# A fused attention and feed-forward kernel: the planner that orders its instructions gets another model of VectorE and GpSimd, new costs and new ranks

## The chip, the core and the metric

The kernel runs on one core of a Trainium2 chip. Its time is the device time of one execution in microseconds (us). The engines are named as the profile names them: PE is TensorE's matmul, PEld its weight load, DVE is VectorE, ACT is ScalarE, POOL is GpSimd, SP is SyncE, which issues most DMAs.

## What is computed

```python
def _attn_ref(q, k, v, n_sink, window):        # (4, 8, 768, 64) each
    scores = np.matmul(q, k.transpose(0, 1, 3, 2)) / np.sqrt(D)
    keep = (pos < n_sink) | ((rel >= 0) & (rel < window))     # 4 sinks, window 128
    scores = np.where(keep, scores, -1e9)
    a = np.exp(scores - np.max(scores, axis=-1, keepdims=True))
    a = a / (np.sum(a, axis=-1, keepdims=True) + 1e-09)
    return np.matmul(a, v)

def _moe_ref(x, w_in, w_out):                  # (3072, 512), (512, 2048), (2048, 512)
    h = np.maximum(x @ w_in, 0.0)
    return (h * h @ w_out).astype(np.float32)
```

The attention's output, with its heads side by side, is the input of the two matrix products.

## The kernel before

The 3072 tokens are cut into eight chunks of 384, two for each batch entry. For each chunk there are four head pairs; one pair of one chunk is one attention step `s` (s = 4 x chunk + pair). An attention step makes scores on PE (line 663 for the first eight steps, 669 with split operands for the others), masks and reduces them on DVE (646, with its accumulator read), takes exponentials on ACT (652), a reciprocal on DVE (712), scales P with it (719, on POOL, ACT or DVE), copies the sink columns into PSK (730 and 732), turns P (by PE, line 849, for chunks 0 and 1; by DVE's 32 x 32 transposes, line 878, and a DMA round trip `via`, lines 889 and 895, for the others) and multiplies with the values (942 and 948). The result is taken out of PSUM as a rounded part `xh` (ACT, 958), a remainder `xl` (DVE, 963) and a 16-bit copy `x16` (515 on POOL, 512 on ACT or DVE).

The products go by columns of 128 of the 2048 hidden units. A column of a chunk has 12 matmuls of the first product (line 1031), then ReLU, square and 16-bit casts on ACT, DVE and POOL (1045, 1050, 1135 or 1133, 512 or 515, and the remainder `gl` on DVE at 1067), then 9 matmuls of the second product (1086 and 1109). The columns are done in nine legs: chunk 0's first 8 columns, chunk 1's 16, chunk 0's other 8, then chunks 2 to 7 with 16 each. So the 33rd column is chunk 2's first.

The weights come as 64-bit numbers in 32 rows. Each row is built into 32-bit and 16-bit parts by three integer steps and one subtraction on DVE (393, 400, 407, 433), a scaling on ACT (428) and a 16-bit cast on POOL, ACT or DVE (441, 512). All this happens while the first two and a half legs run; it is called the building stage here. Chunks 3 to 7 carry side work: their columns reload weights and values in pieces and test their size (`check_steps`, `value_steps`). At the end a few DVE steps form a verdict (`numbers`, `limits`, `within`, `verdict`), which decides whether a general second program has to run.

The order is not written by hand. `Plan.add` records each step with its engine (or a list of engines to choose from), a cost, a rank, what it reads and writes and the PSUM banks it takes. `Plan.order` then simulates the engines: at each point it gives every ready step a start time, picks by time and rank, and emits. A cost of the form `("DVE", 0.62, "port")` marks a DVE operation that shares something with POOL. In the kernel before, a POOL step waits for the marked DVE operation before it (`half`), while a marked DVE operation waits only for a POOL step that carries the mark itself:

```python
                if "port" in kind:
                    t = max(t, port["DVE" if e == "POOL" else "POOL"])
                elif e == "POOL":
                    t = max(t, half)
```

What comes out is a fixed order on each engine; the chip then runs each engine's list in that order, with waits where one needs another.

Of the kernel before, what the change touches and what calls it, by code (L numbers as in the profile page):

```python
# [19 lines left out]
P = 128  # L20
# [4 lines left out]
TOK = 384  # L25
# [9 lines left out]
SHARE = 1.0  # L35
LOW_POOL = 0.57
KLOW_DVE = 0.0
KLOW_POOL = 0.0
HOLD = 0.1
SC_DVE = 0.13  # L40
CLAIM = (True, False)
KS_ACT = 0.01
SOON = 7.71
PS_DVE = 0.19
EARLY = 5
SLOW = 8.5
LAG = 0.77
KEEP = 1.11
STAY = 0.03
LANDS = (3.3, 1.65, 0.6)  # L50
VS_POOL = 3.0
GRAB = 1.9
# [3 lines left out]
URGE = 0.52  # L56
LOW_DVE = 0.0
CP_DVE = 0.47
SC_ACT = 0.26
ROW = 2  # L60
# [5 lines left out]
SHORT_ACT = 0.1  # L66
SHORT_DVE = 0.3
G16_ACT = 0.1
G16_DVE = 0.2
FULL_DVE = 3.0  # L70
# [20 lines left out]
class Plan:  # L91
# [46 lines left out]
    def order(self):  # L138
        free = dict(PE=FIRST, DVE=4.9, ACT=5.1, POOL=5.2, SP=1.7, Q=0.0)
        port, landed, mode, flow, half = {"DVE": 0.0, "POOL": 0.0}, [], 0, 0.0, 0.0  # L140
        open_ = [n for n, s in enumerate(self.steps) if s["waits"] == 0]
        while open_:
            best = {}
            for n in open_:
                s = self.steps[n]
                ready, picks = self.able(s)
                if ready is None:
                    continue
                e, cost, *kind = min(s["at"], key=lambda o: max(ready, free[o[0]]) + o[1] + (o[3] if len(o) > 3 else 0.0))
                t = max(ready, free[e])  # L150
                if e == "SP" and len(landed) > 7:
                    t = max(t, landed[-8])
                if "port" in kind:
                    t = max(t, port["DVE" if e == "POOL" else "POOL"])
                elif e == "POOL":
                    t = max(t, half)
                best.setdefault(e, []).append((t, s["rank"], n, cost, kind, picks))
            chosen = None
            for e, able in best.items():
# [6 lines left out]
                if chosen is None or a[0] < chosen[1][0] or (e == "POOL" and a[0] <= chosen[1][0] + 0.001):  # L166
                    chosen = e, a
            e, (t, rank, n, cost, kind, picks) = chosen
# [15 lines left out]
            else:  # L184
                done = t + cost + self.TAIL[e]
                if "port" in kind:
                    port[e] = t + cost
                    if e == "DVE":
                        half = t + SHARE * cost
# [17 lines left out]
def sink_window_attention_moe(  # L207
# [25 lines left out]
    with ExitStack() as fast:  # L233
# [146 lines left out]
        def row_steps(n, rank):  # L380
# [4 lines left out]
            def load():  # L385
# [6 lines left out]
                ("DVE", 0.345, "port"), rank,  # L392
# [6 lines left out]
                ("DVE", 0.62, "port"), rank,  # L399
# [6 lines left out]
                ("DVE", 0.62, "port"), rank,  # L406
# [6 lines left out]
        def split_steps(n, rank):  # L413
# [6 lines left out]
            def rooms(at):  # L420
# [11 lines left out]
                ("DVE", 0.62, "port"), rank,  # L432
# [6 lines left out]
            def short(e):  # L439
# [4 lines left out]
                [("POOL", 0.65), ("ACT", 0.52, "", SHORT_ACT), ("DVE", 0.36, "port", SHORT_DVE)], rank, short,  # L444
# [6 lines left out]
        def check_steps(n, rank, n_tick):  # L451
# [9 lines left out]
                ("ACT", 0.5), rank,  # L461
# [14 lines left out]
        def scale_steps(fc, rank, n_tick):  # L476

            add(
                ("DVE", 1.2), rank,
# [6 lines left out]
        def value_steps(s, rank, n_tick):  # L486

            half, p = divmod(s, NPAIR)
            kb, nk = 4 * half, 2 if half else 4
# [4 lines left out]
                lambda: nc.sync.dma_start(out=room()[:, 0:nk], in_=v[0, p, :, kb : kb + nk].rearrange("p n x d -> p n (x d)")),  # L494
# [11 lines left out]
        NPS = 2 * NPAIR  # L506
        HALVES = ((0, slice(0, D), slice(D, P)), (1, slice(D, P), slice(0, D)))
# [35 lines left out]
        def attention(s, rank):  # L543
# [68 lines left out]
            if not plain:  # L612
                for h, own, oth in HALVES:
# [3 lines left out]
                        [("DVE", 0.35, "port", 0.0), ("ACT", 0.6 if nk == 4 else 0.5, "", KS_ACT)], r,  # L617
# [18 lines left out]
                        ("DVE", 0.585, "port"), r,  # L636
# [44 lines left out]
            for m, (i, heads) in enumerate(order):  # L681
# [16 lines left out]
                for h, key in zip(heads, keys):  # L698
                    add(
                        ("DVE", 0.355 if n > P else 0.21), r - URGE,  # L700
# [6 lines left out]
                        ("ACT", 0.505 if n > P else 0.385), r - URGE, lambda h=h, i=i, n=n, o=o: exp(h, i, n, o),  # L707
# [27 lines left out]
            for heads in groups:  # L735
# [3 lines left out]
                    ("ACT", 0.2), r - URGE,  # L739
# [802 lines left out]
```

## Time and profile before

| what | before |
|---|---|
| time, median of 3 runs | 653.4 us (653.38 to 653.88) |
| time of the profiled execution | 653.41 us |
| its span from first to last instruction | 651.5 us |
| PE busy | 636.6 us (98%) |
| DVE busy | 483.1 us (74%) |
| ACT busy | 436.2 us (67%) |
| POOL busy | 195.5 us (30%) |
| DMA read and written | 80.29 and 24.38 MB |

The profiled execution is as long as the median. Its time stands 1.9 us over its span. Busy shares are means over stages that have different limits, so they have to be read stage by stage; and PE's ends are modelled, so that a PE that is shown as busy need not be at its full rate.

### The profile page before, as it was taken

What the parts mean: (1) busy time and instruction counts of PE and PEld (TensorE: products, weight loads), DVE (VectorE), ACT (ScalarE), POOL (GpSimd) and SP (SyncE); (2) the same over time, 40 slices, a digit from 0 to 9 for tenths busy, and PEclk for the clock granted to TensorE, in tenths of its full rate; (3) what the DMA queues carried; (4) which work ended last, traced back from release to release, by engine and by line L of the source; (5) the groups of instructions that cost most, each with busy time, mean ns of one, the idle gap of its engine ahead of it and who ended that gap; (6) DMA issues with size and microseconds to landing.
All of it is one profiled execution on the core that took longest, in us unless ns stands there. A gap on an engine that the chain in (4) does not pass through costs nothing.

```text
span 651.5 us, 12170 instructions
## 1 busy us (share of the span) xinstructions
PE 636.6 (98%) x3736; PEld 422.2 (65%) x3736; DVE 483.1 (74%) x1315; ACT 436.2 (67%) x1361; POOL 195.5 (30%) x391
## 2 busy tenths in 40 slices
PE   7989999999999999999999999999999999999995
PEld 6656556665666666666666666666666666666663
DVE  8999999999668676666878776576777888553332
ACT  6998867677675566665568777776777686555421
POOL 4534544636322232323233222333422422000000
PEclk8999999999999999999999999999999999999998
DMA  8636564766766554365677776657667755332001
GB/s 292 219 127 185 173 208 125 232 180 167 198 187 183 127 165 108 92 187 143 181 204 214 217 213 190 197 165 191 187 182 203 222 153 163 116 109 69 17 2 52
DMA packets 85748, 106.53 MB, mean 164 GB/s; under 512 B 12760, under 2 KB 60376, under 8 KB 85676
## 3 DMA queue, kind: packets, MB, share of 16 engines
q1 hardware_dynamic: 85068, 105.05, 55.9%
q8 instruction: 30, 0.49, 0.3%
q10 hardware_dynamic: 576, 0.60, 0.3%
q14 instruction: 42, 0.34, 0.2%
q0 software_dynamic: 32, 0.05, 0.0%
HBM read 80.29 MB, written 24.38 MB: 161 GB/s over the span
## 4 chain that ended last, share of the span: by engine, by line
PE 80%; DVE 12%; ACT 2%; issue 2%; DMA 2%; POOL 1%; SPq 0%; DVEq 0%; ACTq 0%
PE bank L1031 33%; PE bank L1086 23%; PE bank L1109 11%; PE bank L942 5%; PE bank L669 5%; DVE wc L433 2%; DVE f L407 2%; DVE f L400 2%; DVE P L646 1%; PE bank L663 1%; DMA via<-T 1%; DVE f L393 1%; PE bank L948 1%; DVE gc L1067 1%; ACT P L652 1%
## 5 line engine op out<-in xcount | busy, mean ns | idle before, releaser
L1031 PE MATMUL bank<-xc,wc 128*128 128x384 f16 x1024 | 196.2, 327 | 0.6 <-DVE wc L433 0.6
L1031 PE MATMUL bank<-xh,wh 128*128 128x384 f32 x512 | 146.6, 386 | 0.0
L1045 ACT ACTIVATE r<-bank 128x384 f32<-128x384 f32 x128 | 62.6, 489 | 114.6 <-PE bank L1031 89.8
L1031 PEld LDWEIGHTS <-wc 128*128 128x128 f16 x1024 | 90.7, 98 | 67.4 <-issue 9.2
L719 POOL TENSOR_SCALAR P<-P,small 128x260 f32<-128x260 f32 (+1 forms) x158 | 84.8, 551 | 145.0 <-DVE small L712 138.9
L652 ACT ACTIVATE P<-P,nbs 128x260 f32<-128x260 f32 (+1 forms) x192 | 93.2, 486 | 43.6 <-DVE nbs L646 43.1
L1086 PE MATMUL bank<-wc,gc 128*128 128x512 f16 x450 | 110.2, 381 | 0.0
L1135 DVE SCALAR_TENSOR_TENSOR bank<-bank,r 128x384 f32<-128x384 f32 x96 | 54.1, 563 | 63.7 <-ACT r L1045 63.5
L1031 PEld LDWEIGHTS bank<-xh,wh 128*128 128x128 f32 x512 | 90.9, 189 | 13.1 <-ACT P L652 0.3
L1109 PE MATMUL bank<-wc,gc 128*128 128x512 f16 (+1 forms) x350 | 90.9, 364 | 0.4 <-DVE gc L1067 0.4
L646 DVE CUSTOM_DVE_ANT_0 P<-bank,maskA 128x260 f32<-128x260 f32 x128 | 52.6, 420 | 36.4 <-PE bank L669 35.3
L1086 PEld LDWEIGHTS <-gc 128*128 128x128 f16 x450 | 38.0, 98 | 52.8 <-issue 9.4
L1109 PE MATMUL bank<-wh,gh 128*128 128x512 f32 (+1 forms) x175 | 71.4, 445 | 0.2 <-DVE ob L1141 0.2
L1067 DVE TENSOR_TENSOR gc<-bank,gh 128x384 f16<-128x384 f32 x128 | 70.2, 548 | 0.7 <-ACT bank L1133 0.3
L1050 ACT ACTIVATE gh<-r 128x384 fp32r<-128x384 f32 x128 | 66.5, 520 | 3.3
L669 PE MATMUL bank<-KS,QS 128*128 128x260 f32 (+1 forms) x288 | 65.1, 310 | 0.5 <-DVE nbs L646 0.5
L1086 PE MATMUL bank<-wh,gh 128*128 128x512 f32 x225 | 64.8, 396 | 0.0
L669 PEld LDWEIGHTS bank<-KS,QS 128*128 128x128 f32 x288 | 52.2, 189 | 10.0 <-DVE nbs L646 1.2
L878 DVE STREAM_TRANSPOSE T<-P 128x384 f32<-128x384 f32 x96 | 46.8, 495 | 1.8 <-POOL P L719 1.0
L1109 PEld LDWEIGHTS <-gc 128*128 128x128 f16 x350 | 23.9, 98 | 34.6 <-issue 20.7
L515 POOL CAST gc<-gh 128x384 f16<-128x384 f32 x33 | 21.5, 651 | 65.8 <-ACT gh L1050 65.6
L1086 PEld LDWEIGHTS bank<-wh,gh 128*128 128x128 f32 x225 | 38.8, 188 | 3.2
(132 smaller groups left out, 919.2 us busy)
## 6 DMA issues: line engine op xcount, KB each, us to landing
raw<-in_moe_w_dram SPq DMA_DIRECT2D x32, 512.0 KB, 4.3
half<-in_moe_w_dram SPq DMA_DIRECT2D x64, 256.0 KB, 3.1
via<-T SPq DMA_DIRECT2D x96, 96.0 KB, 2.0
PT<-via SPq DMA_DIRECT2D x24, 384.0 KB, 4.2
via<-T SPq DMA_DIRECT2D x96, 80.0 KB, 2.6
PT<-via SPq DMA_DIRECT2D x24, 320.0 KB, 3.8
kn<-in_k_dram SPq DMA_DIRECT2D x28, 264.0 KB, 4.3
qn<-in_q_dram SPq DMA_DIRECT2D x31, 192.0 KB, 3.7
```

The lines of the kernel that those rows point to most:

```text
L646: nc.vector.tensor_tensor_reduce(Pt(h)[:, i, o : o + n], ps_[:, 0:n], mask[:, 0:n], -SCALE, BIG, ALU.add, ALU.min, nb)
L652: nc.scalar.activation(Pt(h)[:, i, o : o + n], Pt(h)[:, i, o : o + n], AF.Exp, bias=nb, scale=-1.0, accum_out=sm[:, h, i : i + 1],)
L669: nc.tensor.matmul(bank(key)[:, 0:n], QS(h)[:, cols], flat[:, a, c0 : c0 + n], start=(a == 0), stop=(a == 1),)
L719: {"POOL": nc.gpsimd, "DVE": nc.vector}[engine].tensor_scalar(a, a, rs[:, h, i : i + 1], 1.0, op0=ALU.mult, op1=ALU.mult)
L878: nc.vector.transpose(dst.rearrange("p c j b -> p j c b"), src.rearrange("p j (c b) -> p j c b", b=32))
L1031: nc.tensor.matmul(bank(key)[:, 0:TOK], wt[:, cols], xt, start=(m == 0 and j == 0), stop=(m == len(runs) - 1 and j == len(run) - 1),)
L1045: lambda key=key, r=r: nc.scalar.activation(r(), bank(key)[:, 0:TOK], AF.Relu, scale=R_SCALE),
L1050: lambda gh=gh, r=r, fc=fc: nc.scalar.activation(gh(), r(), AF.Square, accum_out=gsum[:, c % 2, fc : fc + 1]),
L1067: lambda key=key, gh=gh, gc=gc: nc.vector.tensor_tensor(gc()[:, 1], bank(key)[:, 0:TOK], f32(gh()), op=ALU.subtract),
L1086: nc.tensor.matmul(bank(okey)[:, 0:DM], gt, wt, start=(f == f0 and x == 0), stop=False,)
L1109: nc.tensor.matmul(bank(okey)[:, cols], gt, wt[:, cols], start=(f == f0 and j == 0), stop=(f == f1 - 1 and j == 2),)
L1135: nc.vector.scalar_tensor_tensor(full, full, R_SCALE, r, op0=ALU.mult, op1=ALU.mult)
```

## The change

- `Plan.order` treats every POOL step and every marked DVE operation as excluding each other: either waits for the other's end, and the choice of an engine for a step counts that wait. Where a marked DVE operation is about to follow another one and a POOL step was ready by the time that the first one began, POOL goes first.
- Costs and choice penalties of nearly all steps get new numbers, mostly a few hundredths of a us; the planner's engines begin later (DVE at 5.75 in place of 4.9 us).
- Ranks of the attention steps of chunks 1 to 7, of the rows and of the column's side steps become other numbers (`TWO`, `THREE`, `ROW`, `COLUMN`, `SOON`).
- The size test of chunk 2's values, a DVE reduction in its four attention steps, becomes four `value_steps` in later legs, with a reload by DMA each.
- `numbers`, and with it `limits`, wait for a column 20 before the end in place of nothing.

```diff
@@ constants
-HOLD = 0.1
-SC_DVE = 0.13
+HOLD = 0
+SC_DVE = -0.001
-KS_ACT = 0.01
-SOON = 7.71
-PS_DVE = 0.19
+KS_ACT = 0.37
+SOON = 4.111
+PS_DVE = -0.1
-VS_POOL = 3.0
+VS_POOL = 1.0
-G16_ACT = 0.1
-G16_DVE = 0.2
+G16_ACT = -0.07
+G16_DVE = 0.564
+TWO = (1.596, -1.602, 1.784)
+THREE = (1, 3.951, 0.051, 3.388)
+COLUMN = 14
...
@@ def order(self):
-        free = dict(PE=FIRST, DVE=4.9, ACT=5.1, POOL=5.2, SP=1.7, Q=0.0)
+        free = dict(PE=FIRST, DVE=5.75, ACT=6.1, POOL=6.5, SP=1.7, Q=0.0)
...
+                def begin(o):
+                    t = max(ready, free[o[0]])
+                    if "port" in o or o[0] == "POOL":
+                        t = max(t, port["DVE" if o[0] == "POOL" else "POOL"])
+                    return t
+
+                e, cost, *kind = min(s["at"], key=lambda o: begin(o) + o[1] + (o[3] if len(o) > 3 else 0.0))
+                came = max(ready, free[e])
+                t = begin((e, cost, *kind))
...
-            e, (t, rank, n, cost, kind, picks) = chosen
+            if chosen[0] == "DVE" and "port" in chosen[1][4] and "POOL" in best:
+                waiting = min((a for a in best["POOL"]), key=lambda a: a[:3])
+                if waiting[6] <= held and waiting[0] <= chosen[1][0]:
+                    chosen = "POOL", waiting
+            e, (t, rank, n, cost, kind, picks, came) = chosen
...
@@ def attention(s, rank):
-            if not plain:
+            if s >= RELOAD:
                 add(
-                    ("DVE", 0.08 + 0.125 * nk), rank(1.0),
+                    ("DVE", 0.08 + 0.13 * nk), rank(1.0),
...
-        checks = [(value_steps, x) for x in range(NPS)] + [(check_steps, x) for x in range(2 * NROW)]
+        checks = [(value_steps, x) for x in range(RELOAD)] + [(check_steps, x) for x in range(2 * NROW)]
...
-        add(("DVE", 0.7), END, numbers, reads=[], writes=["checks"])
+        add(("DVE", 0.7), END, numbers, reads=[("tick", item - 20)], writes=["checks"])
```

The first place where the order moves is DVE's list just after the masks are made, in the first 10 us. Line 646 is the masked reduction of the first scores (shown as ISA, with its accumulator read behind it), 1257 to 1269 are `numbers` and `limits`. Before:

```order
L646 ISA P_1_184,nbs<-bank_68,mask_97 128x128
L646 ISA nbs 128x1
L1257 TENSOR_SCALAR par<-parf 128x2
L1258 TENSOR_TENSOR par<-par,parf 128x2
L1259 SCALAR_TENSOR_TENSOR par<-parf,par 128x2
L1260 TENSOR_TENSOR checks<-par,parf 128x2
L646 ISA P_0_180,nbs<-bank_69,mask_95 128x260
L646 ISA nbs 128x1
L646 ISA P_1_184,nbs<-bank_70,mask_95 128x260
L646 ISA nbs 128x1
L1264 TENSOR_SCALAR checks<-parf 128x1
L1265 TENSOR_SCALAR checks<-parf 128x1
```

In the changed kernel the same place (its line numbers are 10 to 12 higher; 658 is the reduction) reads:

```order
L658 ISA P_1_188,nbs<-bank_68,mask_97 128x128
L658 ISA nbs 128x1
L542 CAST VS<-vs_111 24x512
L544 SCALAR_TENSOR_TENSOR VS<-VS,third,vs_111 24x512
L658 ISA P_0_186,nbs<-bank_69,mask_95 128x260
L658 ISA nbs 128x1
L658 ISA P_1_188,nbs<-bank_70,mask_95 128x260
L658 ISA nbs 128x1
```

The nine steps of `numbers` and `limits` are gone from here, and the two steps that make the sink values VS have come to DVE from POOL, where they were three.

The second place is POOL's list from that point to the first 16-bit copy of an attention result. 719 scales P, 732 and 730 copy sink columns into PSK, 515 is the 16-bit copy. Before:

```order
L530 CAST VS<-vs_111 24x512
L536 TENSOR_SCALAR VS<-VS,third 24x512
L537 TENSOR_TENSOR VS<-VS,vs_111 24x512
L719 TENSOR_SCALAR P_0_180<-P_0_180,small 128x128
L719 TENSOR_SCALAR P_1_184<-P_1_184,small 128x128
L732 CAST PSK_wide<-P_0_180 128x2x2x4
L732 CAST PSK_wide<-P_1_184 128x2x2x4
L730 TENSOR_TENSOR PSK_wide<-P_0_180,PSK_wide 128x2x4
L730 TENSOR_TENSOR PSK_wide<-P_1_184,PSK_wide 128x2x4
L719 TENSOR_SCALAR P_230<-P_230,small 128x128
L719 TENSOR_SCALAR P_230<-P_230,small 128x260
L515 CAST xc_162<-xh_161 128x384
```

In the changed kernel POOL has these rows from the same point (731 scales, 744 and 742 are the sink columns, 451 is a row's cast, 527 the 16-bit copy):

```order
L731 TENSOR_SCALAR P_0_186<-P_0_186,small 128x128
L451 CAST wc_325<-wh_316 128x512
L527 CAST xc_162<-xh_161 128x384
L744 CAST PSK_wide<-P_0_235 128x2x2x4
L744 CAST PSK_wide<-P_1_237 128x2x2x4
```

POOL keeps one of four scalings and none of the first step's four sink copies; DVE has them.

The third place is PE's list around the values of chunk 2's third and fourth pair (942 and 948, in the changed kernel 954 and 960). Before, they stand in front of the 30th and 31st column's first product (`xh_161`, chunk 0):

```order
L942 MATMUL bank_67<-PT_165,vn_160 64x256 x4
L942 MATMUL bank_67<-PT_165,vn_160 64x128 x2
L948 MATMUL bank_69<-SK_135,VS 128x256
L1109 MATMUL bank_73<-wh_1415,gh_630 128x512
L1109 LDWEIGHTS gc_641
L1109 MATMUL bank_73<-wc_1440,gc_641 128x512
L1109 LDWEIGHTS gc_641
L1109 MATMUL bank_73<-wc_1440,gc_641 128x512
L1031 MATMUL bank_70<-xh_161,wh_1653 128x384
L1031 LDWEIGHTS wc_1668
```

In the changed kernel they stand behind the last first-product column of chunk 0; the part shown ends with chunk 2's first (`xc_164`, line 1043):

```order
L954 MATMUL bank_68<-PT_165,vn_160 64x128 x2
L960 MATMUL bank_69<-SK_135,VS 128x256
...
L960 MATMUL bank_68<-SK_135,VS 128x256
...
L1121 MATMUL bank_72<-wc_1638,gc_624 128x512
L681 MATMUL bank_69<-KS_1_2225,QS_1_2218 128x260 x2
L681 MATMUL bank_67<-KS_1_2225,QS_1_2218 128x260 x2
L1043 LDWEIGHTS wc_325
L1043 MATMUL bank_71<-xc_164,wc_325 128x384
```

Between the last row of values and chunk 2's first product there were three columns; now there are six matmuls of a second product and four of scores.

## Rows read from the trace of the kernel before

**Rows 1.** Busy time by stretch: start:end, length, then each engine's busy us.

```profile
0.00:20.00 20.00, 16.65 (x92) 13.45 (x93) 17.98 (x80) 13.52 (x48) 8.97 (x28) 0.91 0.79 269
20.00:80.00 60.00, 56.11 (x374) 36.01 (x373) 58.41 (x166) 53.82 (x156) 28.85 (x47) 1.00 0.55 180
80.00:100.00 20.00, 19.57 (x112) 11.53 (x111) 19.88 (x34) 12.63 (x30) 8.27 (x11) 1.00 0.57 182
100.00:160.00 60.00, 59.30 (x335) 36.92 (x334) 59.61 (x154) 44.71 (x132) 30.89 (x51) 1.00 0.64 185
160.00:600.00 440.00, 440.00 (x2567) 294.08 (x2565) 309.58 (x841) 295.54 (x950) 118.50 (x257) 1.00 0.61 169
```

**Rows 2.** Chain of waits from 9 to 165 us: start, length, what.

```profile
9.53 0.06 DVE ones L1269
...
32.00 0.50 DVE P L719 x2
...
33.13 0.09 DVE PSK_wide L732
...
41.70 1.47 POOL PSK_wide L730
...
68.63 0.27 DVE gc L512
...
94.25 0.60 DVE wc L433
...
97.12 0.47 DVE vmax L591
...
160.89 2.03 PE bank L1109 x9
162.92 2.03 PE bank L1031 x12
```

**Rows 3.** DVE's groups by line and shape: count, busy us and mean ns.

```profile
L433 DVE SCALAR_TENSOR_TENSOR wc<-f,wh 128x512 f16<-128x512 f32 x32 | 25.6, 808 | 0.1
L400 DVE SCALAR_TENSOR_TENSOR f<-raw,f 128x512 int32<-128x512 int32 x32 | 23.5, 741 | 0.1
L407 DVE SCALAR_TENSOR_TENSOR f<-raw,f 128x512 int32<-128x512 int32 x32 | 22.6, 715 | 0.1
L393 DVE TENSOR_SCALAR f<-raw 128x512 int32<-128x512 int32 x32 | 14.9, 487 | 0.0
```

**Rows 4.** The same four lines alone: shortest, median and longest in ns.

```profile
L433 DVE SCALAR_TENSOR_TENSOR wc<-f,wh x32: 645/687/1098, 20.4 to 159.2; 128x512 f16<-128x512 f32 x32
L400 DVE SCALAR_TENSOR_TENSOR f<-raw,f x32: 645/682/1092, 15.6 to 153.8; 128x512 int32<-128x512 int32 x32
L407 DVE SCALAR_TENSOR_TENSOR f<-raw,f x32: 651/681/1251, 16.6 to 155.3; 128x512 int32<-128x512 int32 x32
L393 DVE TENSOR_SCALAR f<-raw x32: 379/416/1344, 15.2 to 149.2; 128x512 int32<-128x512 int32 x32
```

**Rows 5.** Timeline of DVE from 6 to 10 us: start, length, what.

```profile
6.36 0.16 DVE L1257 TENSOR_SCALAR par<-parf 128x2 f32<-128x2 f32 x1
...
7.43 0.43 DVE L646 CUSTOM_DVE_ANT_0 P<-bank,mask 128x260 f32<-128x260 f32 x1
...
8.13 0.15 DVE L1264 TENSOR_SCALAR checks<-parf 128x1 f32<-128x1 f32 x1
...
9.55 0.43 DVE L646 CUSTOM_DVE_ANT_0 P<-bank,maskA 128x260 f32<-128x260 f32 x1
```

**Rows 6.** ACT's groups by line and shape, the 16-bit casts.

```profile
L512 ACT CAST gc<-gh 128x384 f16<-128x384 f32 x20 | 10.2, 509 | 0.6
L512 ACT CAST wc<-wh 128x512 f16<-128x512 f32 x9 | 5.5, 612 | 0.2
```

**Rows 7.** DMA issues of chunks' first halves: KB each, median us to landing.

```profile
via<-T SPq DMA_DIRECT2D x96, 80.0 KB, 2.6
PT<-via SPq DMA_DIRECT2D x24, 320.0 KB, 3.8
```

More of the change, by code (lines that the diff above doesn't have):

```diff
@@ L138, in order @@
     def order(self):
-        free = dict(PE=FIRST, DVE=4.9, ACT=5.1, POOL=5.2, SP=1.7, Q=0.0)
-        port, landed, mode, flow, half = {"DVE": 0.0, "POOL": 0.0}, [], 0, 0.0, 0.0
+        free = dict(PE=FIRST, DVE=5.75, ACT=6.1, POOL=6.5, SP=1.7, Q=0.0)
+        port, landed, mode, flow, held = {"DVE": 0.0, "POOL": 0.0}, [], 0, 0.0, -1.0
         open_ = [n for n, s in enumerate(self.steps) if s["waits"] == 0]
@@ L148, in order @@
                     continue
-                e, cost, *kind = min(s["at"], key=lambda o: max(ready, free[o[0]]) + o[1] + (o[3] if len(o) > 3 else 0.0))
-                t = max(ready, free[e])
+                def begin(o):
[6 more added lines that the diff above has]
+                t = begin((e, cost, *kind))
                 if e == "SP" and len(landed) > 7:
                     t = max(t, landed[-8])
[L153 to L157, printed above, removed]
+                best.setdefault(e, []).append((t, s["rank"], n, cost, kind, picks, came))
             chosen = None
@@ L185, in order @@
                 done = t + cost + self.TAIL[e]
-                if "port" in kind:
+                if "port" in kind or e == "POOL":
                     port[e] = t + cost
-                    if e == "DVE":
-                        half = t + SHARE * cost
+                if e == "DVE":
+                    held = t if "port" in kind else -1.0
             for key in s["drop"]:
@@ L391, in row_steps @@
             add(
-                ("DVE", 0.345, "port"), rank,
+                ("DVE", 0.336, "port"), rank,
                 lambda: nc.vector.tensor_scalar(
@@ L398, in row_steps @@
             add(
-                ("DVE", 0.62, "port"), rank,
+                ("DVE", 0.603, "port"), rank,
                 lambda: nc.vector.scalar_tensor_tensor(
@@ L405, in row_steps @@
             add(
-                ("DVE", 0.62, "port"), rank,
+                ("DVE", 0.603, "port"), rank,
                 lambda: nc.vector.scalar_tensor_tensor(
@@ L431, in split_steps @@
             add(
-                ("DVE", 0.62, "port"), rank,
+                ("DVE", 0.603, "port"), rank,
                 lambda: nc.vector.scalar_tensor_tensor(
@@ L443, in split_steps @@
             add(
-                [("POOL", 0.65), ("ACT", 0.52, "", SHORT_ACT), ("DVE", 0.36, "port", SHORT_DVE)], rank, short,
+                [("POOL", 0.58), ("ACT", 0.51, "", SHORT_ACT), ("DVE", 0.35, "port", SHORT_DVE)], rank, short,
                 reads=[("w", n)], writes=[("w16", n)] + rooms(2 * fc + 1),
@@ L635, in attention @@
                     add(
[L636 removed]
+                        ("DVE", 0.565, "port"), r,
                         lambda h=h, own=own, oth=oth: nc.vector.tensor_tensor(
```

89 lines of the change are left out of this document (45 added, 44 removed).

## The prediction

> **What bounds the kernel now.** I read the busy time by stretch first, because the page's shares are means. From 160 to 600 us PE is busy all of the time while DVE has 309.58 of 440 us and ACT 295.54 [rows 1]: there only PE's own work counts, and counted in the built programs PE's matmuls are the same before and after, but for 6 more short filling matmuls. What a new order can win or lose is therefore what PE loses ahead of 160 us, and a new wait behind it. Up to 100 us PE is idle 20 - 16.65, 60 - 56.11 and 20 - 19.57, 7.7 us together, and in these stretches DVE is the full engine: 58.41 of 60 and 19.88 of 20 us. From 100 to 160 us PE and DVE are both nearly full (0.70 and 0.39 us idle) [rows 1]. The chain of waits says the same: from 9.53 us on it runs through DVE, with pieces on POOL and ACT, nearly without a break to 100 us [rows 2]. So in the building stage a microsecond of DVE is about a microsecond of the end; behind it DVE work costs nothing.
>
> Then I asked what DVE's time there is made of. The four steps that build a row take 808, 741, 715 and 487 ns in the mean [rows 3], but their shortest take 645, 645, 651 and 379 [rows 4]. The excess, 32 x (0.163 + 0.096 + 0.064 + 0.108), is 13.8 us; the longest of them last 1.1 to 1.3 us [rows 4]. POOL is busy 77.0 us in the same 160 us [rows 1], and in the timeline the long ones lie beside POOL's operations. That is 0.18 us of DVE lost for each us of POOL.
>
> **Term 1, the start.** `numbers` and `limits` run on DVE between the first reductions: from 6.36 to the next reduction at 7.43 and from 8.13 to the one at 9.55 [rows 5], 1.07 + 1.42 = 2.49 us, and the chain goes through their last step at 9.53 [rows 2]. They move to the last 22 columns, where DVE is idle for 30% of the time [rows 1]; were DVE full there, they would cost the same 2.49. In their place DVE makes VS, a cast and a two-input step on rows of 512. I price the second as the row's subtraction, 0.60 from start to start in the chain, and the first as two scalings of 260, 0.25 each [rows 2], together 1.1 us. Term 1: -1.4 us.
>
> **Term 2, POOL's work and what DVE loses to it.** I counted both programs up to DVE's ninth `gl` step (line 1067), which stands near 94 us. POOL has 84 instructions ahead of it before and 48 after: VS gone, 12 row casts down to 8, 16-bit copies 11 to 5, scalings 14 to 7, sink copies 22 to 10. At the mean length of POOL's instructions up to 100 us (46.1 us over 86, 0.54 us [rows 1]) 36 fewer are 19.3 us, 42%. The loss up to 100 us, 0.18 x 46.1 = 8.3 us, falls by as much if loss follows work: -3.5 us. Bounds: nothing, if the remaining POOL steps meet DVE as before in sum; -8.3, if the order keeps all marked steps apart. I take -3.5, since the order fixes lists and not times.
>
> The Trainium skill speaks to this (SBUF — State Buffer, section Who interferes with whom): GpSimd and a DVE instruction that reads two SBUF tensors, or runs in a two-port mode, exclude each other for the whole instruction. The longest durations above agree with it. The same section says that issue order decides who is blocked, which speaks against a planner that fixes lists and not times: by it the sum would lose term 2 and stand at 654.1.
>
> **Term 3, what DVE does in addition.** Ahead of the same point DVE gets 11 more scalings at 0.25, 12 more sink copies at 0.09 [rows 2], and by the count one subtraction and one row step more, 0.8: +4.6. It loses four 16-bit casts of 0.27 and a value reduction of 0.47 [rows 2]: -1.6. Sum: +3.0. The sink copies that go to DVE free PE of waits like that for POOL's 1.47 us at 41.70, which is in the chain; three such steps at 0.09 in their place give -1.2. DVE is idle 1.6 us from 20 to 80 us [rows 1], so no more than that is to be had here. Term 3: +1.8.
>
> **Term 4, ACT.** ACT takes 7 column casts and 5 row casts more ahead of that point, 7 x 0.51 + 5 x 0.61 [rows 6], 3 copies of a result at the same 0.51, and gives up 6 scalings at about 0.45: +5.4 us. From 20 to 80 us it is idle for 60 - 53.82 = 6.2 us [rows 1]. The work fits, barely; two full engines that wait for each other lose something. Bounds 0 and 5.4; I take +1.0, nearer to nothing because the idle time is larger than the work.
>
> **Term 5, from 100 to 160 us.** PE's 0.70 us of idle time [rows 1] goes, and its chain through DVE loosens: chunk 2's attention stands later, and up to the last built row POOL has 82 rows in its list in place of 137, DVE 8 fewer casts, two value reductions fewer and 7 fewer score reductions. By the excess of 0.18 a us on POOL's 30.89 us, a third fewer is -1.8; the matmul that ends the wait is PE's own for part of the time, so I take -1.5 (bounds 0 and -1.8 - 0.7).
>
> **Term 6, the way into chunk 2.** Before, chunk 2's last values stand three columns ahead of its first product. Now they stand right in front: behind them PE has six matmuls of a second product and four of scores, near 1.8 us, while ACT and DVE still have to take two results out. And in front of them the DMA round trip must have ended: from the last transposes there are 16 second-product, 24 first-product and 6 score matmuls, by the chain's 2.03 us for 12 of the first or 9 of the second product [rows 2] and some 0.1 a score matmul 3.6 + 4.1 + 0.6 = 8.3 us, against five issues (0.42 each in the kernel's own costs), 2.6 for `via` and 3.8 for its way back [rows 7], 8.5. It is a draw. I take +0.8; bounds 0 and the whole return, 3.8.
>
> **At nothing.** Four reloads of values with four reductions fill slots 73 to 76 of 80 in the later legs: SP has its DMA queue busy 0.61 there and DVE 30% free [rows 1]; without that cover each is one reduction of half a us. Of DVE's 75 column casts 67 lie behind the building stage; they go to ACT and POOL, 56 in all to ACT at 0.51, 28 us on top of 295.54 of 440 [rows 1]. The filling matmuls stand where PE waits; bound 6 x 0.2 us.
>
> **The sum.** -1.4 - 3.5 + 1.8 + 1.0 - 1.5 + 0.8 = -2.8 us. From the profiled execution's 653.41 us, which is also the median, that is **650.6 us**.
>
> **Rivals.**
> A. *ACT takes the place of DVE.* For it: 53.82 of 60 us are busy, and 5.4 us come on top of 6.2 idle [rows 1]. Against: after 80 us ACT is idle over a third of the time and can catch up. It decides from the point where the added work ahead of the ninth column outgrows the 6.2 us, or where ACT stands idle early and has none left. If PE then waits for all 5.4 us and the row-building gains lie in DVE's shade, only terms 1 and 6 stay: 653.4 - 1.4 + 0.8 + 5.4 = 658; with half of it 655.5. Slower. Chance 0.09.
> B. *The way into chunk 2 costs its whole return*, 3.8 in place of 0.8: 653.6. It needs DVE's last transposes to come where the list puts them and not earlier. Chance 0.08.
> C. *The lists do not bring POOL and DVE apart*, since their times drift, and the blocking falls as before on DVE: 650.6 + 3.5 = 654.1, or with half of it 652.4. For it: nothing ties POOL's start to DVE's. This is what the Trainium skill's rule on issue order, above, would make of the change. Against: there is simply less POOL work. Chance 0.12.
> D. *The order keeps them apart.* Then term 2 is up to -8.3: 645.8; with two thirds of it 648.6. Chance 0.2 for 645.5 to 648.6.
> E. Forecast, 648.6 to 652.1: chance 0.48. Below 645.5: 0.03.
>
> **The numbers.** About 0.2% (1.3 us) is what a measurement can tell from no change, so faster is below 652.1. E, D and the lowest give 0.71, and a third of C 0.04: faster 0.75. The same, to 654.7, take most of B and C: 0.14. Slower keeps A and some of B: 0.11. The range runs from 645.6, D's end, to 654.0, which leaves out A and the ends of B and C, near 0.17 in all.
>
> **What would show it.** In the changed profile: no DVE step of `numbers` before 500 us, and the first reductions 1.4 us earlier (term 1); means of the four row steps near 0.75, 0.70, 0.69 and 0.44, and POOL's busy time up to 100 us near 27 (term 2); DVE still over 95% busy to 80 us with ACT over 95% beside it, and no large wait of DVE for ACT (term 4); PE full from about 95 us (term 5); one PE wait of about 1 us near 200 us ahead of chunk 2's first product (term 6). The prediction is wrong if ACT rather than DVE ends most waits from 20 to 80 us, or if PE's idle time up to 100 us stays at 7.7 us.

## The result, and the profile after

The changed kernel takes 646.59 us (median of 5 runs, 646.45 to 646.89) against 653.40 us for the kernel before on the same chip: a ratio of 0.9895, 95% interval 0.9881 to 0.991. The forecast was 650.6 us, a gain of 2.8 us; 6.8 us came. The time lies inside the range, close to its lower end.

The busy time by stretch, as in [rows 1] (start:end, length, then PE, PEld, DVE, ACT, POOL, the granted clock, DMA):

```profile
0.00:20.00 20.00, 17.77 (x113) 15.03 (x113) 18.34 (x85) 14.76 (x53) 5.08 (x18) 1.00 0.84 293
20.00:80.00 60.00, 59.55 (x401) 38.13 (x399) 59.67 (x182) 58.27 (x166) 12.76 (x27) 1.00 0.59 183
80.00:100.00 20.00, 20.00 (x105) 11.46 (x104) 19.90 (x37) 15.65 (x37) 3.91 (x3) 1.00 0.67 218
100.00:160.00 60.00, 60.00 (x342) 37.87 (x341) 53.43 (x143) 47.90 (x138) 26.17 (x44) 1.00 0.59 161
160.00:600.00 440.00, 440.00 (x2575) 294.58 (x2573) 303.14 (x851) 299.26 (x964) 111.47 (x238) 1.00 0.61 170
```

PE's idle time up to 100 us is 2.23 + 0.45 + 0 = 2.7 us where it was 7.7, and from 100 to 160 us nothing where it was 0.70. POOL's busy time up to 100 us is 5.08 + 12.76 + 3.91 = 21.75 us where it was 46.1: 48 instructions of 0.45 us in place of 86 of 0.54. DVE is as full as before from 20 to 80 us, and ACT has gone from 53.82 to 58.27 of 60 us.

The four steps that build a row, as in [rows 3] (line, count, busy us, mean ns), and then their shortest, median and longest, as in [rows 4]; the lines 433, 407, 400 and 393 of before are 443, 417, 410 and 403 now:

```profile
L443 DVE SCALAR_TENSOR_TENSOR wc<-f,wh 128x512 f16<-128x512 f32 x32 | 23.0, 723 | 0.0
L417 DVE SCALAR_TENSOR_TENSOR f<-raw,f 128x512 int32<-128x512 int32 x32 | 21.9, 689 | 0.0
L410 DVE SCALAR_TENSOR_TENSOR f<-raw,f 128x512 int32<-128x512 int32 x32 | 21.7, 683 | 0.0
L403 DVE TENSOR_SCALAR f<-raw 128x512 int32<-128x512 int32 x32 | 13.3, 426 | 0.0
```

```profile
L443 DVE SCALAR_TENSOR_TENSOR wc<-f,wh x32: 649/680/1112, 19.7 to 145.2; 128x512 f16<-128x512 f32 x32
L417 DVE SCALAR_TENSOR_TENSOR f<-raw,f x32: 661/681/945, 15.5 to 139.7; 128x512 int32<-128x512 int32 x32
L410 DVE SCALAR_TENSOR_TENSOR f<-raw,f x32: 650/680/783, 14.5 to 139.0; 128x512 int32<-128x512 int32 x32
L403 DVE TENSOR_SCALAR f<-raw x32: 374/417/824, 14.0 to 135.8; 128x512 int32<-128x512 int32 x32
```

The shortest are within 10 ns of what they were; the means fell. The excess, 32 x (0.074 + 0.028 + 0.033 + 0.052), is 6.0 us where it was 13.8.

The start of DVE's timeline, as in [rows 5], with VS where `numbers` stood:

```profile
6.37 0.41 DVE L542 CAST VS<-vs 24x512 fp32r<-24x512 f32 x1
6.81 0.74 DVE L544 SCALAR_TENSOR_TENSOR VS<-VS,third,vs 24x512 fp32r<-24x512 f32 x1
7.48 0.41 DVE L658 CUSTOM_DVE_ANT_0 P<-bank,mask 128x260 f32<-128x260 f32 x1
...
8.17 0.41 DVE L658 CUSTOM_DVE_ANT_0 P<-bank,maskA 128x260 f32<-128x260 f32 x1
```

The first reduction under `maskA` starts at 8.17 us where it started at 9.55 [rows 5].

The chain of waits, its shares by engine, and its pieces around the way into chunk 2 (L1121 is the second product, L1043 the first, L954 the product with the values):

```profile
PE 94%; DVE 2%; ACT 1%; DMA 1%; issue 0%; SPq 0%; DVEq 0%
...
186.17 2.03 PE bank L1043 x12
188.19 2.31 PE bank L954 x24
...
193.71 2.01 PE bank L1043 x12
```

From 33 us on it runs on PE alone but for the output's last step. Before, it came back to DVE up to 157 us: added up over its pieces from 9.53 to 100 us, DVE had 46.7 us, PE 18.9, ACT 13.9 and POOL 4.8. Chunk 2's values and the first product behind them stand in it without a wait.

### The profile page after: what moved, and what is told of

Same layout as the page of the kernel before. It is cut to its first block, busy times and chain, and to the rows that moved or that the text cites. A ratio compares the mean times of both kernels' runs of the same rounds, so it can differ in the third digit from the quotient of the medians.

```text
span 644.6 us, 12246 instructions
## 1 busy us (share of the span) xinstructions
PE 635.0 (99%) x3748; PEld 422.5 (66%) x3748; DVE 467.2 (72%) x1322; ACT 455.4 (71%) x1413; POOL 159.4 (25%) x330
## 4 chain that ended last, share of the span: by engine, by line
PE 94%; DVE 2%; ACT 1%; DMA 1%; issue 0%; SPq 0%; DVEq 0%
PE bank L1043 40%; PE bank L1098 23%; PE bank L1121 17%; PE bank L954 6%; PE bank L681 5%; PE bank L960 1%; PE bank L675 1%; ACT P L664 1%; PE bank L861 1%; DVE P L658 1%; DMA qn<-in_q_dram 1%; DVE wc L443 0%; DVE f L417 0%; PE bank L789 0%; DVE P L731 0%; DVE xc L975 0%
## 5 line engine op out<-in xcount | busy, mean ns | idle before, releaser
L1043 PE MATMUL bank<-xc,wc 128*128 128x384 f16 x1024 | 195.3, 327 | 0.0
L1043 PE MATMUL bank<-xh,wh 128*128 128x384 f32 x512 | 142.1, 377 | 0.0
L1043 PEld LDWEIGHTS <-wc 128*128 128x128 f16 x1024 | 92.9, 98 | 72.3 <-issue 9.9
L731 POOL TENSOR_SCALAR P<-P,small 128x260 f32<-128x260 f32 (+1 forms) x151 | 74.0, 506 | 150.7 <-DVE small L724 134.8
L1043 PEld LDWEIGHTS bank<-xh,wh 128*128 128x128 f32 x512 | 89.2, 189 | 10.6 <-ACT xh L970 0.3
L1121 PE MATMUL bank<-wc,gc 128*128 128x512 f16 (+1 forms) x350 | 90.2, 363 | 0.0
L1121 PE MATMUL bank<-wh,gh 128*128 128x512 f32 (+1 forms) x175 | 70.3, 443 | 0.0
L527 POOL CAST gc<-gh 128x384 f16<-128x384 f32 x52 | 26.6, 512 | 158.1 <-ACT gh L1062 146.9
L681 PE MATMUL bank<-KS,QS 128*128 128x260 f32 (+1 forms) x288 | 61.8, 305 | 0.0
L681 PEld LDWEIGHTS bank<-KS,QS 128*128 128x128 f32 x288 | 50.2, 189 | 7.8
L1121 PEld LDWEIGHTS <-gc 128*128 128x128 f16 x350 | 24.2, 98 | 34.3 <-issue 20.6
L1098 PEld LDWEIGHTS bank<-wh,gh 128*128 128x128 f32 x225 | 40.4, 188 | 3.2
```

The lines of the kernel that those rows point to most:

```text
L681: nc.tensor.matmul(bank(key)[:, 0:n], QS(h)[:, cols], flat[:, a, c0 : c0 + n], start=(a == 0), stop=(a == 1),)
L731: {"POOL": nc.gpsimd, "DVE": nc.vector}[engine].tensor_scalar(a, a, rs[:, h, i : i + 1], 1.0, op0=ALU.mult, op1=ALU.mult)
L1043: nc.tensor.matmul(bank(key)[:, 0:TOK], wt[:, cols], xt, start=(m == 0 and j == 0), stop=(m == len(runs) - 1 and j == len(run) - 1),)
L1098: nc.tensor.matmul(bank(okey)[:, 0:DM], gt, wt, start=(f == f0 and x == 0), stop=False,)
L1121: nc.tensor.matmul(bank(okey)[:, cols], gt, wt[:, cols], start=(f == f0 and j == 0), stop=(f == f1 - 1 and j == 2),)
```

## The experiments

The theory to test was my own sum: the steps that leave DVE early are worth about 3 us (2.49 of `numbers` and `limits`, 0.47 of a reduction), and the planner's new lists about nothing in sum, since what POOL gives back (-3.5) is used up by DVE's extra work, ACT and the way into chunk 2. The rivals: all of it is the early steps; the lists give much more than I said; what I gave to DVE is the granted clock at the start. All runs are against the kernel before on the same chip; the interval is that of the ratio. The runs were made on several chips, on which the kernel before took 653.01 to 653.83 us, so two runs are compared by what each gained or lost against its own kernel before.

### The two halves of the change

The kernel before with one line of the change (e1), and with the value reductions moved too (e2):

```
-        add(("DVE", 0.7), END, numbers, reads=[], writes=["checks"])
+        add(("DVE", 0.7), END, numbers, reads=[("tick", item - 20)], writes=["checks"])
...
-            if not plain:
+            if s >= RELOAD:
```

> The kernel before with one edit: numbers waits for a late column (with limits behind it); value reductions, planner, costs and ranks as before. Theory D (DVE is the full engine to 100 us, and each us taken off it is a us of the end): the 2.49 us of these steps, so 650.5 us (650.2 to 651.2), and what the late value reductions add (the run with both gave 649.6) is about 1 us. Theory R (the gain of the late steps is a lucky new order): anywhere from 649 to 653 us with no such sum.

> The kernel before with only the late steps of the change: numbers waits for a late column, and the value reductions of chunks 0 to 2 run late on reloaded values; planner, costs and ranks as before. Theory S (the planner's lists give most of the 6.8 us): only my first term, 1.4 us, and two reductions of 0.47 us that leave the full DVE are had, so 651.1 us (650.4 to 652.2), and the excess of the four row steps stays near 13.8 us. Theory L (taking work off DVE early gives most): 647.5 to 649.5 us, with PE's idle time up to 100 us down to 3 to 4 us.

Measured: e1 649.78 us, 0.9947 (0.9933 to 0.996); e2 649.60 us, 0.9949 (0.9936 to 0.9963). So the late `numbers` alone give 3.4 us, more than the 2.49 us that its steps took (e1 lies just below Theory D's range), and the value reductions, to which Theory D gave about 1 us, add nothing that shows.

The changed kernel with these edits taken back, the planner kept (e3):

> The changed kernel with the late steps undone: numbers at the start again and value reductions of chunks 2 and later inside the attention; planner, costs and ranks as changed. Theory S: loses the first term and the two reductions, 646.6 + 1.4 + 0.9 = 648.9 us (648 to 649.6), with POOL busy about 22 us up to 100 us and an excess of the row steps near 6 us. Theory L: 651 to 652.5 us.

Measured: 649.58 us, 0.9946 (0.9933 to 0.996), with an excess of the row steps of 5.9 us and POOL busy for 26.0 us up to 100 us. So the planner alone gives 3.4 us as well, and the two gains add up. e3 ends where Theory S has it, e2 between the theories: neither half is most of the gain.

### Lock and constants apart

The planner's loop of before in the changed kernel (e4), and the new loop, in which POOL steps and marked DVE operations exclude each other (the lock), in the kernel before (e5):

> The changed kernel, its costs and ranks and late steps kept, with the planner's loop of before (a marked DVE step holds POOL, but a POOL step does not hold a marked DVE step; engines free from 4.9 to 5.2 us). Theory S1 (the lock is what keeps POOL's work out of the building stage): POOL's list is longer by 41 rows, so up to 100 us it is busy 30 us or more, the excess of the row steps is near 9 to 10 us, and the time 649.5 to 651.5 us. Theory S2 (the re-fitted costs and ranks do it): 646.5 to 647.5 us with an excess near 6 us.

> The kernel before with only the planner's loop of the change (lock both ways, later start of the engines); costs, ranks and early steps as before. Theory S1: POOL's list is shorter by 30 rows, its busy time up to 100 us falls from 46 to 30 us or less, the excess from 13.8 to 9 us or less, and the time to 649 to 651 us. Theory S2: with the old costs the lock plans wrongly and the time is 652.5 to 655 us.

Measured: e4 659.05 us, 1.009 (1.0075 to 1.0106); e5 661.31 us, 1.0122 (1.0107 to 1.0138). Each part alone makes the kernel slower; of the theories only S2 of e5 had the sign, and none the size. In e4 POOL is busy for 42.2 us up to 100 us, and PE idles though DVE is full:

```profile
20.00:80.00 60.00, 54.96 (x367) 34.56 (x367) 59.86 (x172) 49.94 (x143) 25.53 (x42) 1.00 0.55 176
```

In e5 POOL has 31.6 us, near the 30 that Theory S1 had, and the excess is 7.1 us, but PE waits at some places for more than a microsecond, and behind such a wait its granted clock stands at 0.50, that is 1.2 GHz:

```profile
26.00:28.00 2.00, 0.92 (x7) 0.77 (x7) 1.82 (x6) 2.00 (x6) 0.26 (x1) 1.00 0.84 255
28.00:30.00 2.00, 0.87 (x4) 0.29 (x2) 2.00 (x6) 1.69 (x5) 1.66 (x2) 0.72 0.85 275
30.00:34.00 4.00, 3.52 (x16) 3.12 (x17) 2.41 (x14) 2.44 (x7) 0.46 (x3) 0.50 0.30 117
...
166.00:167.00 1.00, 1.00 (x4) 0.64 (x3) 0.97 (x4) 0.92 (x2) 0.67 (x1) 0.50 0.00 0
```

Which constants does the loop need? e11 is the changed kernel with the ranks and rules of choice of before:

```
-SOON = 4.111
+SOON = 7.71
...
-TWO = (1.596, -1.602, 1.784)
+TWO = (2, 1, 2.2)
...
```

e12 is it with the durations and penalties of before, and e16 with both of before (that is e2 with the new loop):

```
-SHORT_ACT = 0.347
+SHORT_ACT = 0.1
...
-                ("DVE", 0.336, "port"), rank,
+                ("DVE", 0.345, "port"), rank,
...
```

> The changed kernel with the ranks and the planner's rules of choice of before (SOON, TWO, THREE, COLUMN, ROW, GRAB, LAG, KEEP, STAY, URGE, HOLD) and the new durations, penalties for an engine, lock and late steps. Theory T (what made the lock alone cost 8.3 us is the old durations and penalties, which give POOL and DVE the wrong work): 646.5 to 649 us. Theory O (it is the old ranks, under which attention and columns stand in the wrong order for the lock): 652 us or more, with stretches in which PE waits and its granted clock falls to 0.5.

> The counterpart: lock, late steps and the new ranks and rules of choice, with the durations and engine penalties of before. Theory T: 652 us or more. Theory O: 646.5 to 649 us. Its POOL list has 345 rows where the changed kernel's has 306, so by contention alone (0.3 us of DVE a us of POOL, were 20 of the 39 rows in the building stage) it would lose 3 us: 649.5 us.

> The kernel before with the planner's new loop and the late steps, costs and ranks as before. Additive: 661.3 - 3.4 = 657.9 us (657 to 659). If the lock's loss came from the early steps that stand in DVE's way: 650 to 653 us, with no stretch at a granted clock of 0.5.

Measured: e11 649.27 us, 0.9942 (0.9928 to 0.9955); e12 649.92 us, 0.9952 (0.9938 to 0.9966); e16 655.16 us, 1.0031 (1.002 to 1.0043). In us against the kernel before, with the late steps in all of them:

| | costs and ranks of before | new costs, old ranks | old costs, new ranks | both new |
|---|---|---|---|---|
| loop of before | -3.4 (e2) | | | +6.0 (e4) |
| loop with the lock | +2.0 (e16) | -3.8 (e11) | -3.1 (e12) | -6.8 |

The lock by itself costs 5.4 us, each half of the re-fit gives about that back (5.7 and 5.1), and only both give 3.4 us on top. Theories T and O both missed: e11 lies just above T's range and e12 just above O's, while each had 652 us or more for the other run. e16 also shows that the lock's loss in e5 is only partly due to the early steps (the additive 657.9 us was 2.7 too high); its granted clock still falls, to 0.94 from 20 to 80 us.

### What POOL's work costs

In the kernel before, with its lists, POOL's casts write half the elements and its scalings 32 columns (e9):

```
-                nc.gpsimd.tensor_copy(dst, src) if e == "POOL" else copy(e, dst, src)
+                half_copy(dst, src) if e == "POOL" else copy(e, dst, src)
...
+            nc.gpsimd.tensor_copy(dst.bitcast(F32), src[:, 0:n])
...
-                a = Pt(h)[:, i, o : o + n]
+                a = Pt(h)[:, i, o : o + (32 if engine == "POOL" and s < 2 * NPS else n)]
```

> The kernel before, its lists unchanged, with POOL's work in the building stage made smaller: POOL's casts write half as many elements and its scalings only 32 columns, so the output is not the reference's, and the flag of the general program is held at zero. Theory P (DVE's loss beside POOL sets the end): POOL's busy time up to 100 us falls from 46 to about 28 us, the excess of the row steps from 13.8 to 8 or 9 us, and the time to 648 to 650 us. Theory K (the loss is hidden, and the order of the lists is what counts): 652 to 653 us.

Measured: 647.94 us, 0.9916 (0.9902 to 0.9929), 5.2 us faster with no instruction moved. POOL fell only to 37.1 us up to 100 us, the excess to 9.1 us. PE went from 56.11 to 58.22 us busy in the stretch, and DVE's row subtraction, by line and shape, from 808 to 716 ns [rows 3]:

```profile
20.00:80.00 60.00, 58.22 (x395) 37.56 (x393) 58.37 (x170) 56.58 (x162) 20.85 (x48) 1.00 0.59 189
```

```profile
L433 DVE SCALAR_TENSOR_TENSOR wc<-f,wh 128x512 f16<-128x512 f32 x32 | 22.7, 716 | 0.0
```

So POOL's work is worth these 5.2 us of the end, as Theory P has it. That all of it is DVE's loss isn't shown: the edit also shortens what others wait for. In the chain of waits up to 100 us POOL's pieces add up to 4.8 us in the kernel before and to 1.0 in e9. The longest of them before, beside the 1.47 us of [rows 2]:

```profile
12.57 0.50 POOL P L719
22.58 1.41 POOL wc L441
23.98 0.58 POOL P L719
```

The counterpart: 21 more POOL copies in the changed kernel (e7).

```
+                if e == "POOL" and not any(x.startswith("ob_") for x in made):
+                    for _ in range(3):
+                        nc.gpsimd.tensor_copy(sb("ob1", [P, WR], F16, "scratch"), src)
```

> The changed kernel with 21 more POOL copies of 128x512 in the building stage (three behind each of 7 row casts, into a scratch room that nobody reads), about 12 us more of POOL's time, all lists else as they were. Theory P (what POOL does costs DVE 0.125 to 0.18 us a us, and DVE is still the full engine): the excess of the row steps rises from 6.0 to 7.5 to 8.2 us, the time to 648.1 to 648.8 us. Theory N (PE is the full engine now from 32 us on and has room): 646.6 to 647.2 us although the excess rises.

Measured: 655.86 us, 1.004 (1.0027 to 1.0054), 9.5 us slower than the change, far beyond Theory P. The excess rose to 9.1 us, 3.1 more for 13 us more of POOL. The rest has another cause, which PE's waits from 28 to 45 us (us, times, longest) and the stretches show: POOL's scalings of P now stand behind the copies, PE waits for them, and the granted clock falls.

```profile
PE bank L864 <- POOL P L734: 2.9, 2, 2.6
```

```profile
34.00:36.00 2.00, 0.12 (x2) 0.13 (x2) 0.30 (x3) 0.00 (x0) 1.69 (x4) 1.00 0.08 31
36.00:38.00 2.00, 2.00 (x12) 1.62 (x13) 1.98 (x9) 1.61 (x5) 0.00 (x0) 0.71 0.00 0
38.00:40.00 2.00, 2.00 (x8) 1.16 (x7) 1.71 (x6) 1.18 (x4) 0.00 (x0) 0.50 0.03 8
```

The run therefore doesn't measure contention alone; it shows that a POOL list with little in it is also worth its short way to P.

### ACT

The row copy of ACT made twice for 12 rows, in the changed kernel (e8) and in the kernel before (e15):

```
-                ("ACT", 0.52), rank, lambda: nc.scalar.activation(wh()[:, x], f32(f()), AF.Copy, scale=scale),
+                ("ACT", 0.52), rank, lambda: [
+                    nc.scalar.activation(wh()[:, x], f32(f()), AF.Copy, scale=scale)
+                    for _ in range(2 if 8 <= n < 20 else 1)
+                ],
```

> The changed kernel with ACT's 128x512 copy of 12 rows (8 to 19) made twice, some 12 x 0.53 = 6.4 us more of ACT in the stretch from about 20 to 80 us, where it has 58.27 of 60 us busy; all lists else unchanged. Theory A (my fourth term: ACT and DVE are interlocked and ACT has no room left): the time rises by 4 to 6.5 us, to 650.5 to 653 us. Theory N (PE is the full engine from 32 us on and ACT runs ahead of it): 646.5 to 647.5 us.

> The kernel before with ACT's 128x512 copy of rows 8 to 19 made twice, 6.4 us more of ACT, the same edit that cost the changed kernel 5.3 us. Theory A (my fourth term: 6.2 us of idle time on ACT is room that can be filled): 653 to 654.5 us. Theory I (the interlock of ACT and DVE costs as much before): 656 to 659 us.

Measured: e8 651.93 us, 0.9983 (0.9974 to 0.9992), 5.7 us slower than the change; e15 656.13 us, 1.0046 (1.0032 to 1.006), 2.9 us slower than before. In e8 the stretch and DVE's waits from 20 to 100 us (us, times, longest) show the interlock:

```profile
20.00:80.00 60.00, 58.38 (x388) 36.49 (x384) 56.39 (x175) 58.72 (x165) 12.24 (x27) 1.00 0.55 175
```

```profile
DVE wc L446 <- ACT wh L439: 3.7, 8, 0.8
```

So ACT has no room for this work in the changed kernel, and about half the room before: 6.2 us of idle time took in only about half of 6.4 us of work. Theory A of e8 is right. e15 lies at the low end of Theory I's range, but the loss is half of e8's and not as much. Both runs put the second copy right ahead of the subtraction that waits for it (in e15 DVE waits 2.1 us there), so they test ACT's room at this place, and not for a cast that nothing waits for.

### The clock at the start

In [rows 1] the granted clock is 0.91 from 0 to 20 us, in the changed kernel 1.00; in the finer trace of before it is 0.50 (1.2 GHz) from 13 to 16 us, behind PE's idle 0.79 us from 12 to 13. e6 gives the kernel before 16 filling matmuls in place of 8:

```
-WARM = (12.0, 24.0)
+WARM = (8.0, 24.0)
-FULL = 0.75
+FULL = 1.0
...
-                if picks and WARM[0] < t < WARM[1] and t > free[e] + 0.4:
+                if picks and WARM[0] < t < WARM[1] and t > free[e] + 0.3:
```

e14 takes all of them from the changed kernel:

```
-FULL = 0.75
+FULL = 0
```

> The kernel before with 16 filling matmuls in place of 8 ahead of 24 us (the window, the gap and the share at which the planner fills are changed, nothing else), so that PE's granted clock should stay at 1.00 where it was 0.50 from 13 to 16 us. Theory C (the dip at the start, 3.4 us at half clock, 1.7 us of PE's work, is a part of the gain): 651.3 us (650.8 to 652). Theory D (DVE sets the end there and PE's dip lies in its shade): 653 us, within 0.5.

> The changed kernel without any filling matmul, lists else unchanged. If a dip of the granted clock at the start counts: a stretch at 0.50 between 9 and 20 us, and up to 1.7 us more, 648.3 us. If DVE sets the end there (as when fills were added to the kernel before, which changed nothing): 646.6 us, within 0.5.

Measured: e6 653.34 us (652.70 to 654.67), 1.0006 (0.9997 to 1.0015), at a granted clock of 1.00 in all 20 us, and its fastest run lies within 0.1 us of the fastest of before (652.78); e14 646.91 us, 0.9903 (0.9888 to 0.9919), as fast as the change, although its clock fell behind two idle microseconds:

```profile
11.00:12.00 1.00, 0.06 (x1) 0.00 (x0) 1.00 (x7) 1.00 (x6) 0.00 (x0) 1.00 0.84 291
12.00:13.00 1.00, 0.00 (x0) 0.00 (x0) 1.00 (x8) 1.00 (x5) 0.33 (x1) 1.00 1.04 389
...
15.00:16.00 1.00, 0.75 (x4) 0.29 (x2) 1.00 (x4) 1.00 (x4) 0.00 (x0) 0.50 1.05 388
```

DVE is full beside it, in each of these rows 1.00 of 1.00 us. So the clock at the start is no part of the gain that shows.

### The way into chunk 2, and the start

The ranks of chunk 2's and later attention back to before (e10):

```
-SOON = 4.111
+SOON = 7.71
...
-THREE = (1, 3.951, 0.051, 3.388)
+THREE = (2.0, 4.0, 0.3, 3.2)
```

VS back to POOL (e13):

```
-VS_POOL = 1.0
+VS_POOL = 3.0
```

The penalties of before for the first two attention steps and four rows (e17), or the first step and two rows (e18):

```
-                                pool, ("ACT", 0.4 if n > P else 0.31, "", SC_ACT),
+                                pool, ("ACT", 0.4 if n > P else 0.31, "", SC_ACT if s >= 2 else 0.26),
...
```

> The changed kernel with only the ranks of chunk 2's and later attention as before (SOON 7.71, THREE 2.0, 4.0, 0.3, 3.2). Theory B (chunk 2's attention, pulled ahead, takes DVE and PE time from the building stage): 647.5 to 650 us, lost ahead of 160 us. Theory U (the ranks of chunk 2 do not matter, the way into it is hidden either way): 646.3 to 647.2 us.

> The changed kernel with VS_POOL at 3.0 as before, so that the planner gives VS back to POOL, 2.6 us there, in place of a cast and a two-input step on DVE of 0.41 + 0.74 us each time. Theory V (my first term priced VS on DVE at 1.1 us of the end): PE loses about 1 us less up to 25 us and the time is 645.5 us (645 to 646.2). Theory W (a long POOL step between the first steps costs DVE as much as it saves): 646.5 to 648 us.

> The changed kernel with the engine penalties of before (scalings, sink copies, 16-bit row casts) for the first two attention steps and the first four rows alone, so that POOL takes that work there. If the new penalties hurt the start, PE loses up to 2.4 us less ahead of 25 us: 644.2 to 646.0 us. If the start is set by loads and the first chain, or POOL's work costs DVE as much as it gives: 646.4 to 648.5 us.

> The same for the first attention step and the first two rows alone. By the first reading 645 to 646.2 us, by the second 646.4 to 648 us.

Measured: e10 647.89 us, 0.9919 (0.9906 to 0.9933), lost where Theory B has it, between 100 and 160 us, where PE is busy for 59.05 us:

```profile
100.00:160.00 60.00, 59.05 (x335) 37.05 (x333) 56.86 (x155) 50.96 (x147) 25.09 (x38) 1.00 0.65 177
```

e13 647.96 us, 0.9924 (0.991 to 0.9937): slower than the change, so VS on DVE isn't a loss against VS on POOL. e17 648.05 us, 0.9912 (0.9899 to 0.9926) and e18 649.52 us, 0.9936 (0.9923 to 0.995): no better start was to be had by giving POOL its first work back, and e18 lost more than either reading had. No run beat the changed kernel.

## Why the prediction had the direction and not the size

**The reading of the chain**, on which all terms rest, was too simple: "through DVE nearly without a break to 100 us" holds for 46.7 of 90.5 us. POOL had 4.8 us of it, of which the sum priced the one piece of 1.47 (in term 3); in the changed kernel's chain there is none.

**Term 1** (-1.4) was right in its parts: VS takes DVE from 6.37 to 7.48, 1.1 us as priced, and the first `maskA` reduction comes 1.38 us earlier. The late `numbers` alone gave 3.4 us in e1 where the term had 2.49; why 0.9 more isn't settled. In e1 the first `maskA` reduction starts at 7.24 us where it started at 9.55, and with POOL's work as before (45.0 us up to 100 us) the excess of the row steps fell to 9.4 us and POOL's pieces in the chain to 1.1.

**Term 2** (-3.5) is the step that failed. It let the loss follow POOL's work: 36 fewer instructions at 0.54 us are 19.3 us of POOL, 42%, and 0.18 x 46.1 = 8.3 us of loss falls by as much; that the order could keep the engines apart it set aside, "since the order fixes lists and not times". Measured up to 100 us, POOL fell by 24.3 us, 53%: the instructions that stay are shorter too, 0.45 us. Summed over the row steps that start there, what each takes beyond the shortest of its line, the loss was 8.9 us and is 3.8: -5.1 in place of -3.5. And of this, what is lost beside a POOL instruction fell from 7.5 to 1.4 us, by 82%. In every run with the loop of before 35 to 43 row steps stand beside a POOL instruction, in every one with the lock 6 to 23, with the old costs too. POOL's work is less there as well, but that alone doesn't do it: e9 has 43 such steps at 37.1 us of POOL without the lock, and e16 against e2 has 36% less of POOL and 74% less loss (up to 100 us; row steps that overlap a POOL instruction, of those that start; their excess; POOL's busy time):

| | loop | row steps beside POOL | their excess, us | POOL, us |
|---|---|---|---|---|
| before | of before | 42 of 82 | 7.5 | 46.1 |
| e1 | of before | 35 of 88 | 4.7 | 45.0 |
| e2 | of before | 40 of 89 | 6.4 | 45.7 |
| e4 | of before | 43 of 80 | 6.7 | 42.2 |
| e9 | of before | 43 of 86 | 5.0 | 37.1 |
| e16 | with the lock | 21 of 79 | 1.7 | 29.4 |
| e3 | with the lock | 23 of 91 | 2.0 | 26.0 |
| e11 | with the lock | 11 of 87 | 2.9 | 20.5 |
| change | with the lock | 11 of 91 | 1.4 | 21.75 |

So fixed lists did keep them apart, far better than the term allowed. (In e11 few steps overlap, but two stand beside POOL steps of 1.2 and 1.5 us and take 1.5 us each.) It isn't enough for a gain: e16 has it and is 5.4 us slower than e2. And the term counted four lines only; e9 shows that DVE's scalings lose as well (438 to 354 ns in the mean).

**Term 3** (+1.8) can't be seen apart at the end. DVE's ninth `gl` step ends at 87.4 us where it ended at 93.7, with 278 of DVE's steps in the trace ahead of it in place of 265: the extra work is there (by their durations 4.3 us of scalings and sink copies, priced at 3.8), and is outweighed.

**Term 4** (+1.0) was nothing in the changed kernel. DVE waits for PE alone (0.2 us) from 20 to 100 us, with ACT at 58.27 of 60. But the reason I gave, that the idle time is larger than the work, isn't enough: in e15, without new lists, half of 6.4 us in 6.2 us of idle time lands on the end. That the re-fitted plan placed the work better is likely, and not shown by a run.

**Term 5** (-1.5): PE is full, as forecast, and the row steps that start from 100 to 160 us lose 2.2 us in place of 4.9, 2.7 less. But the term was too large: PE was busy for 59.30 of these 60 us, so no more than its 0.70 us of idle time could come of it, and each half of the change alone brings that (60.00 of 60 us in e1 and in e3).

**Term 6** (+0.8) was nothing: no wait stands ahead of chunk 2's first product. e10, with chunk 2's ranks of before, loses 1.5 us, but ahead of 160 us and not there.

Split by halves, the forecast had -2.49 - 0.47 for the late steps and +0.2 for the planner; measured were -3.4 and -3.4. Of the planner's 3.6 us that I missed, 1.6 are term 2's row steps and 1.8 the waits of terms 4 and 6 that didn't come; term 5 takes 0.8 of this back. The rest, 1.0, stays open, and POOL's pieces that left the chain are one candidate. None of this split is a proof, since the lists change together and e4 and e5 show that their parts don't add.

**The rivals.** A didn't come, but e8 shows its mechanism: 6.4 us of ACT more, and it decides. B didn't come. C's condition, that the lists don't bring the engines apart, did not hold: 11 of 91 row steps beside POOL, and 42 of 82 before. The 654.1 us that the prediction gave it did not come. D is what came, in its mechanism up to 100 us and in its range, with what is lost beside POOL down from 7.5 to 1.4 us; I gave it 0.2. (The range's end of 645.6 lies between the 645.8 of D's sum and the 645.5 of its chance.) From 100 to 160 us the loss fell too, from 4.9 to 2.2, but there e2 has 2.1 with the loop of before. "What would show it" held for the early reductions, DVE, ACT and PE; POOL's 21.75 us against "near 27" was the sign that term 2 was too small.

## What to carry to other kernels

Price the work of a second engine that slows the steps beside it by all that it costs: its own time, which holds waits as well and shrinks with it (POOL's 16-bit row casts up to 100 us: 796 ns in the median before, 616 after), the waits for what it makes, and the loss of every step beside it, not of the four largest lines. And count how many steps stand beside it at all: an order that keeps the two engines apart changes that number, and the loss with it. A planner's model and its constants are one thing: the model with the lock and old constants lost 5.4 us, the new constants with the old model 9.5, and the pair won 3.4. Idle time of an engine in a stretch need not be room: 6.4 us put into 6.2 us of it, right ahead of a step that waits for them, cost 2.9 us of the end.

## What the hardware showed that was not expected

A step of `limits` on one column takes 151 ns late in the run, where no POOL step stands beside it, and took 1136 ns at the start. The line alone, in the kernel before and in e1 (count, shortest/median/longest ns, first and last start):

```profile
L1266 DVE TENSOR_TENSOR checks<-parf x1: 1136/1136/1136, 8.3 to 8.3; 128x1 f32<-128x1 f32 x1
```

```profile
L1266 DVE TENSOR_TENSOR checks<-parf x1: 151/151/151, 561.5 to 561.5; 128x1 f32<-128x1 f32 x1
```

In the trace of before POOL's last step of VS stands beside it, from 8.12 to 9.38 us, and it ends at 9.40. So at least 1.0 of the 2.49 us of term 1 was POOL's. The Trainium skill (SBUF — State Buffer, section Who interferes with whom) has a DVE step with two SBUF inputs and a GpSimd step that reads SBUF exclude each other; the trace agrees, 151 against 1136 ns, and shows that the smallest step pays as much as a large one: it lost 0.98 us, and the most that a row step lost is 1.344 - 0.379 = 0.97 [rows 4].

Beside DVE's marked steps POOL's copies get longer as well: in e7 a copy of 128x512 took 0.62 us, and one 1.07 us (in the chain of waits), which stands beside a row step of DVE (0.67 us from 29.52):

```profile
29.60 1.07 POOL scratch L454
30.73 0.62 POOL scratch L454
```
